# A cosine-attention and token/channel-mixer kernel: the first batch's k loads on ACT's DMA queue, with a rearranged order list

## The chip, the cores and the metric

The kernel runs on one core of a Trainium2 chip. The core has a matrix engine (TensorE, PE in the profile, with its weight loads as PEld), VectorE (DVE), ScalarE (ACT), GpSimd (POOL) and SyncE (SP), which here issues DMA transfers and does nothing else. The metric is the device time of one execution in microseconds. Before the change three runs gave 263.96, 264.58 and 265.01; the median is 264.58 us.

## What is computed

Eight batches of 8 heads, 576 positions, 64 features per head. First a linear attention with cosine weights, then a token mixer and a channel mixer with a residual. The reference, cut to what matters:

```python
def phi(x, c, s):                       # c, s: cos and sin of pi/2 * pos / S
    r = np.maximum(x, 0.0)
    return np.concatenate([r * c, r * s], axis=-1)
q_p = phi(q, cos_w, sin_w); k_p = phi(k, cos_w, sin_w)
kv = np.einsum('bhsf,bhsd->bhfd', k_p, v)
z = np.sum(k_p, axis=2)
num = np.einsum('bhsf,bhfd->bhsd', q_p, kv)
den = np.einsum('bhsf,bhf->bhs', q_p, z)[..., None] + 1e-06
x = (num / den)                          # heads side by side: (8, 576, 512)

xt = x.transpose(0, 2, 1)
h = np.maximum(xt @ w_tok1, 0.0) @ w_tok2
u = x + h.transpose(0, 2, 1)
out = u + np.maximum(u @ w_ch1, 0.0) @ w_ch2
```

## The kernel before

The program is a list, `PLAN` (line 21 on), of 1189 items, carried out from first to last while the program is built. Each item calls a small function with its arguments; a letter names the engine: A for ACT, V for DVE, G for POOL, Y for SP. Every engine works through its own instructions in the order of this list and waits where a result is not there yet. So the list sets the order of each engine and of each DMA queue, and which engine does an elementwise step.

The 576 positions of a batch are nine to each of 64 rows; odd and even partitions hold different parts of them. `load_part(b, name, par, eng, h0, h1)` (line 369) loads batch b of q, k or v for the even (par 0) or odd (par 1) partitions, for heads h0 to h1, with one DMA from the queue of `eng`. For batch 0 each of q, k and v comes in four loads: two parts, each for heads 0 to 3 (the first half) and 4 to 7 (the second half), of 320 KB for part 0 and 256 KB for part 1. For later batches a load covers all 8 heads.

For a batch the steps are:

- `feat` and `rfeat` (lines 389 and 395): relu of q and k with a cosine, sine or tangent factor, into `qp` and `kp`; `vcast` and `vcast_half`: v to bf16. Batch 0 does these by halves of the heads.
- `q_half_mm`, `q_half_out` (batch 0) turn q by TensorE and copy it; later batches use `q_turn_mm`/`q_turn_out` or the DMA transpose `q_turn` from SP.
- `kv_half`, `kv_half_out` and `num_half`, or `kv`, `kv_out`, `num`: the two attention products. `x_hadd`, `x_hrec`, `x_hmul` (or `x_add`, `x_rec`, `x_mul`, all on DVE) divide by the denominator.
- `b1_half`, `uT_x`, `uT_h`, `uT_out` (batch 0) or `b1`, `u_mm`, `u_out`, `u_cast`, `u_turn`: the token mixer. `u_mm(b, c)` makes half of u, `u_out` adds x, `u_cast` makes bf16, and the DMA transpose `u_turn` brings it to the layout for the channel mixer. Batch 0 gets that layout from TensorE (`uT_*`), and its `u_mm` serves the residual.
- `m1(g, s)` (line 805) and `m1_out`: the first channel product of group g, 12 slices of 4 matmuls with 512 columns. `m2` for group 0, and `h_sum`, `prod`, `quarter`, `seed` for the others: the second product with seven partial products in place of eight. Groups 0 to 7 are the batches; group 8 gathers the ninth positions (`tail_*`).

In the list the work of batch b+1 (features, attention, token mixer) lies between the channel products of group b. `warm(n)` (line 588) multiplies a tile of zeros into a PSUM bank n times; its result is not used. There are 28 such items with n = 2.

The weights come by `wtok_part(0..4)` (line 560, the two token matrices), `wc1_load` (line 563) and `wc2_load` (line 582), all from SP, and are cast to bf16 by `w1_cast`, `w2_perm`, `w2t_perm`, `wc1_cast`, `wc2_cast`.

One load of batch 0 is not in the list: the first half of k part 1 goes out on ACT's queue in the setup (line 505), ahead of ACT's table load and of the cosine and sine tables (lines 529 and 530). The other eleven loads of batch 0 are in the list, on SP, in this order: q part 0, k 0, q 1, v 0, v 1 (first halves), q 1, q 0, k 1, k 0, v 0 (second halves), then two token weight parts, v 1 (second half), two more token weight parts, a first piece of `wc1`, and the last token weight part.

Of the kernel before, what the change touches and what calls it, by code (L numbers as in the profile page):

```python
# [21 lines left out]
    ("warm", 2), ("warm", 2), ("warm", 2), ("load_part", 0, "q", 0, "Y", 0, 4), ("load_part", 0, "k", 0, "Y", 0, 4),  # L22
    ("feat", 0, "k", 0, 0, "V", 0, 4), ("feat", 0, "k", 0, 2, "V", 0, 4), ("feat", 0, "q", 1, 4, "A", 0, 4),
    ("feat", 0, "k", 1, 4, "V", 0, 4), ("load_part", 0, "q", 1, "Y", 0, 4), ("rfeat", 0, "q", 4, 5, "A", 0, 4),
    ("load_part", 0, "v", 0, "Y", 0, 4), ("load_part", 0, "v", 1, "Y", 0, 4), ("warm", 2), ("warm", 2),
    ("vcast_half", 0, 3, "G"), ("warm", 2), ("load_part", 0, "q", 1, "Y", 4, 8), ("feat", 0, "k", 1, 3, "A", 0, 4),
    ("feat", 0, "k", 0, 3, "V", 0, 4), ("q_half_mm", 0, 2), ("feat", 0, "q", 1, 1, "V", 0, 4),
    ("rfeat", 0, "q", 2, 4, "A", 0, 4), ("warm", 2), ("load_part", 0, "q", 0, "Y", 4, 8), ("warm", 2), ("warm", 2),
    ("warm", 2), ("feat", 0, "k", 1, 2, "V", 0, 4), ("feat", 0, "k", 0, 1, "A", 0, 4),
    ("feat", 0, "k", 1, 1, "A", 0, 4), ("feat", 0, "q", 1, 3, "V", 0, 4), ("vcast_half", 0, 1, "V"),  # L30
    ("load_part", 0, "k", 1, "Y", 4, 8), ("vcast_half", 0, 2, "G"), ("load_part", 0, "k", 0, "Y", 4, 8),
    ("rfeat", 0, "q", 0, 2, "A", 0, 4), ("warm", 2), ("feat", 0, "q", 1, 0, "V", 0, 4), ("q_half_mm", 0, 0),
    ("load_part", 0, "v", 0, "Y", 4, 8), ("q_half_out", 0, 2, "V"), ("wtok_part", 4),
    ("feat", 0, "q", 1, 2, "V", 0, 4), ("warm", 2), ("warm", 2), ("warm", 2), ("feat", 0, "k", 1, 0, "A", 0, 4),
    ("warm", 2), ("feat", 0, "k", 0, 4, "V", 0, 4), ("feat", 0, "q", 1, 1, "V", 4, 8), ("q_half_out", 0, 0, "V"),
    ("q_half_mm", 0, 1), ("feat", 0, "k", 0, 0, "V", 4, 8), ("wtok_part", 2), ("warm", 2), ("warm", 2),
    ("rfeat", 0, "q", 4, 5, "V", 4, 8), ("feat", 0, "k", 1, 3, "V", 4, 8), ("feat", 0, "q", 1, 2, "A", 4, 8),
    ("vcast_half", 0, 0, "A"), ("kv_half", 0, 0), ("kv_half", 0, 1), ("load_part", 0, "v", 1, "Y", 4, 8),
    ("vcast_half", 1, 1, "G"), ("kv_half", 0, 2), ("kv_half", 0, 3), ("vcast_half", 0, 4, "V"), ("kv_half", 0, 4),
    ("rfeat", 0, "q", 2, 4, "A", 4, 8), ("feat", 0, "k", 0, 2, "A", 4, 8), ("feat", 0, "q", 1, 4, "A", 4, 8),  # L40
    ("feat", 0, "q", 1, 0, "V", 4, 8), ("feat", 0, "k", 0, 3, "A", 4, 8), ("feat", 0, "k", 1, 2, "A", 4, 8),
    ("rfeat", 0, "q", 0, 2, "V", 4, 8), ("q_half_mm", 1, 0), ("wtok_part", 0), ("wtok_part", 1),
    ("w1_cast", 2, 4, "G"), ("warm", 2), ("feat", 0, "q", 1, 3, "A", 4, 8), ("q_half_out", 0, 1, "V"),
    ("q_half_mm", 1, 2), ("feat", 0, "k", 0, 4, "V", 4, 8), ("kv_half_out", 0, "V"), ("num_half", 0, 2),
    ("feat", 0, "k", 0, 1, "A", 4, 8), ("w2t_perm", 1, "V"), ("q_half_out", 1, 0, "V"), ("vcast_half", 1, 0, "V"),
    ("wc1_load", 0, 0, 256), ("num_half", 0, 1), ("num_half", 0, 0), ("wtok_part", 3), ("q_half_mm", 1, 1),
    ("vcast_half", 1, 2, "V"), ("feat", 0, "k", 1, 4, "V", 4, 8), ("w1_cast", 4, 5, "G"), ("vcast_half", 1, 3, "V"),
    ("warm", 2), ("wc1_load", 2), ("warm", 2), ("warm", 2), ("w2_perm", 1, 1, "V"), ("x_hadd", 0, 2),
    ("x_hadd", 0, 0), ("w1_cast", 0, 2, "G"), ("x_hadd", 0, 1), ("w2_perm", 0, 0, "A"), ("wc1_load", 1),
    ("x_hrec", 0, 1), ("feat", 0, "k", 1, 0, "A", 4, 8), ("kv_half", 1, 0), ("feat", 0, "k", 1, 1, "V", 4, 8),  # L50
    ("kv_half", 1, 1), ("kv_half", 1, 2), ("x_hrec", 0, 0), ("kv_half", 1, 3), ("q_half_out", 1, 1, "A"),
    ("x_hmul", 0, 0), ("load_part", 1, "k", 0, "Y"), ("wc1_cast", 8, "G"), ("vcast_half", 1, 4, "A"),
    ("kv_half", 1, 4), ("x_hmul", 0, 1), ("warm", 2), ("warm", 2), ("kv_half_out", 1, "A"), ("num_half", 1, 0),
    ("num_half", 1, 1), ("load_part", 1, "k", 1, "Y"), ("x_hrec", 0, 2), ("x_hmul", 0, 2), ("x_hadd", 1, 0),
    ("x_hrec", 1, 0), ("w2_perm", 1, 0, "G"), ("x_hadd", 1, 1), ("q_half_out", 1, 2, "A"), ("num_half", 1, 2),
    ("x_hadd", 1, 2), ("x_hrec", 1, 1), ("x_hrec", 1, 2), ("warm", 2), ("x_hmul", 1, 0), ("b1_half", 0, 0),
    ("w2_perm", 0, 1, "G"), ("b1_half", 0, 1), ("b1_half", 0, 2), ("b1_half", 0, 3), ("b1_half", 0, 4),
    ("b1_half", 1, 0), ("uT_x", 0), ("b1_half_out", 0, "A"), ("wc1_cast", 0, "A"), ("wc1_load", 0, 256, 512),
    ("wc1_cast", 10, "A"), ("b1_half", 1, 1), ("x_hmul", 1, 1), ("b1_half", 1, 2), ("load_part", 1, "q", 1, "Y"),
    ("uT_x", 2), ("b1_half", 1, 3), ("x_hmul", 1, 2), ("wc1_cast", 7, "A"), ("uT_x", 1), ("b1_half", 1, 4),  # L60
    ("uT_h", 0), ("b1_half_out", 1, "V"), ("wc1_cast", 9, "V"), ("wc1_cast", 1, "G"), ("uT_h", 1), ("uT_x", 3),
    ("uT_h", 3), ("uT_out", 0, "A"), ("load_part", 1, "q", 0, "Y"), ("uT_h", 2), ("wc1_cast", 11, "G"),
    ("uT_out", 1, "A"), ("uT_out", 2, "V"), ("u_mm", 0, 1), ("w2t_perm", 0, "V"), ("load_part", 1, "v", 0, "Y"),
    ("u_out", 0, 1), ("uT_out", 3, "A"),

    ("m1", 0, 7), ("load_part", 1, "v", 1, "Y"), ("m1_out", 0, 7, "V"), ("m1", 0, 1), ("feat", 1, "k", 1, 1, "V"),
    ("m1", 0, 9), ("wc1_cast", 4, "A"), ("feat", 1, "k", 0, 3, "A"), ("feat", 1, "k", 1, 3, "A"),
    ("wc1_cast", 5, "V"), ("feat", 1, "k", 1, 4, "A"), ("feat", 1, "k", 1, 0, "V"), ("m1_out", 0, 9, "V"),
    ("wc1_cast", 3, "G"), ("m1", 0, 11), ("m1_out", 0, 11, "V"), ("feat", 1, "k", 0, 1, "V"), ("m1_out", 0, 1, "A"),
    ("wc1_cast", 6, "G"), ("u_mm", 0, 0), ("m1", 0, 10), ("u_out", 0, 0), ("m1_out", 0, 10, "V"), ("wc2_load", 0),  # L70
    ("wc1_cast", 2, "G"), ("wc2_load", 1), ("feat", 1, "k", 0, 0, "A"), ("m1", 0, 5), ("vcast", 1, 0, "G"),
    ("feat", 1, "k", 1, 2, "A"), ("m1_out", 0, 5, "A"), ("m1", 0, 2), ("vcast", 1, 4, "G"), ("vcast", 1, 3, "G"),
# [214 lines left out]
def kernel(  # L287
# [17 lines left out]
    P = 128  # L305
# [4 lines left out]
    HH = H // 2  # L310
# [7 lines left out]
    A, V, G, SY = nc.scalar, nc.vector, nc.gpsimd, nc.sync  # L318
# [3 lines left out]
    def sb(name, shape, dt):  # L322
        return const.tile(shape, dt, name=name)
# [586 lines left out]
```

## Time and profile before

| | |
|---|---|
| median of the timed runs | 264.58 us (263.96 to 265.01) |
| profiled execution, its own time | 266.13 us |
| span of that execution in the profile | 264.4 us |
| mean granted TensorE clock | 0.992 of full speed |
| first `m1` matmul | 29.23 us |
| last matmul issued | 259.33 us, with 1.47 us to the end of its group of 12 |
| HBM read / written | 35.85 MB / 9.44 MB |

The profile is a record of one execution. Its page gives for each engine the busy time, for 40 slices of the span the busy share, and the groups of instructions with the idle time before them and what ended it. The trace behind it can be asked for single stretches, in order of time or as busy sums, and for the chain that ended last: that is followed back from the last instruction, at each step to whatever released it. "Idle time before" counts only time directly before an instruction. A line number of a helper (such as 373 for all `load_part` DMAs, or 379 for all casts) stands for many callers, so tile names tell them apart. The 40 slices (6.6 us each) for PE, the clock and the DMA engines are:

```
PE   7599999999999999999999999999999999999994
PEclk9899999999999999999999999999999999999999
DMA  5979999989999999999999999658534133200315
```

### The profile page before, as it was taken

The page shows a single profiled execution, that of the slowest core. Times are in us where ns is not written, and L with a number is a line of the kernel's source. Part 1 is how long each engine was busy: PE and PEld are TensorE (multiplying, and loading weights), DVE is VectorE, ACT ScalarE, POOL GpSimd, SP SyncE. Part 2 cuts the span into 40 slices and gives each one's busy share as a digit, 9 for nine tenths or more (in the row PEclk, how much of TensorE's full clock was granted, in tenths as well). Part 3 has the DMA queues.
Part 4 walks back from the last instruction along what each step waited for, and adds up shares of the span by engine and source line. Part 5 has one row for each costly group of instructions (what it writes and reads, how often), then busy time and mean ns, then how long its engine had stood idle before and what let it go on. Part 6 is the DMA issues. An engine that isn't in the chain of part 4 may idle for free.

```text
span 264.4 us, 5482 instructions
## 1 busy us (share of the span) xinstructions
PE 253.9 (96%) x2105; PEld 161.4 (61%) x2122; DVE 193.2 (73%) x400; ACT 130.9 (50%) x224; POOL 92.8 (35%) x100
## 2 busy tenths in 40 slices
PE   7599999999999999999999999999999999999994
PEld 3267456545458655774577457755775575567583
DVE  4677898787699587678898859679956775462574
ACT  3565876881598087855715862387212321222310
POOL 5114315169519201850740224421620160243030
PEclk9899999999999999999999999999999999999999
DMA  5979999989999999999999999658534133200315
GB/s 175 340 281 328 387 398 383 376 214 147 329 356 246 176 319 379 207 209 299 317 278 183 288 236 318 143 191 221 120 87 110 64 70 90 94 9 2 119 45 195
DMA packets 81818, 57.70 MB, mean 218 GB/s; under 512 B 50304, under 2 KB 76544, under 8 KB 81792
## 3 DMA queue, kind: packets, MB, share of 16 engines
q1 hardware_dynamic: 81088, 56.57, 77.3%
q10 hardware_dynamic: 704, 0.79, 0.9%
q8 instruction: 16, 0.26, 0.4%
q14 instruction: 10, 0.08, 0.1%
HBM read 35.85 MB, written 9.44 MB: 171 GB/s over the span
## 4 chain that ended last, share of the span: by engine, by line
PE 68%; DMA 17%; DVE 7%; ACT 3%; issue 3%; SPq 2%; DVEq 0%; ACTq 0%
PE psM L809 26%; PE psM L455 25%; DMA q_raw<-in_q_dram 5%; PE psA L754 5%; DMA u_sb<-in_moe_w_ch_dram 4%; PE psA L766 4%; DMA qpT<-qp 4%; PE psA L715 2%; DMA h1T<-in_moe_w_tok_dram 2%; PE psA L729 2%; DMA uT<-u_bf 2%; SPq L373 2%; ACT kp L401 1%; ACT qp L401 1%; DVE h1T L385 1%
## 5 line engine op out<-in xcount | busy, mean ns | idle before, releaser
L809 PE MATMUL psM<-uT,w_ch 128*128 128x512 bf16 x384 | 89.1, 379 | 0.4 <-ACT h1T L383 0.3
L383 ACT ACTIVATE h1T<-psM 128x512 bf16<-128x512 f32 x67 | 38.5, 595 | 60.5 <-PE psM L809 53.2
L809 PEld LDWEIGHTS <-w_ch 128*128 128x128 bf16 x432 | 40.7, 98 | 43.6 <-issue 0.4
L444 POOL TENSOR_TENSOR h1s<-h1T,h1s 128x512 bf16<-128x512 bf16 (+1 forms) x17 | 28.4, 1675 | 50.5 <-ACT h1T L383 44.2
L455 PEld LDWEIGHTS <-h1s 128*128 128x128 bf16 x384 | 37.2, 98 | 7.1 <-DVE h1s L444 0.2
L467 DVE TENSOR_TENSOR u_sb<-psM,u_sb 128x512 f32<-128x512 f32 x42 | 28.2, 683 | 17.7 <-PE psM L455 17.5
L379 POOL CAST vb<-v_raw 128x512 bf16<-128x512 f32 (+1 forms) x22 | 14.6, 694 | 56.0 <-DMA v_raw<-in_v_dram 50.5
L385 DVE TENSOR_SCALAR h1T<-psM 128x512 bf16<-128x512 f32 x41 | 27.6, 683 | 7.7 <-PE psM L809 7.3
L455 PE MATMUL psM<-w_ch2t,h1s 128*128 128x256 bf16 x276 | 33.1, 273 | 0.0
L455 PEld LDWEIGHTS <-h1T 128*128 128x128 bf16 x288 | 27.6, 98 | 5.4
L401 ACT ACTIVATE qp<-q_raw,tan_t 128x512 bf16<-128x512 f32 (+1 forms) x32 | 21.7, 689 | 10.2 <-DMA q_raw<-in_q_dram 5.9
L770 DVE TENSOR_TENSOR u_sb<-psA,x_sb 128x1024 f32<-128x1024 f32 x16 | 19.2, 1218 | 6.1 <-PE psA L766 3.7
L455 PE MATMUL psM<-w_ch,h1T 128*128 128x256 bf16 x192 | 23.6, 273 | 0.0
L744 DVE TENSOR_TENSOR x_sb<-psA,rden 128x512 bf16<-128x512 f32 x28 | 19.0, 685 | 0.6
L401 ACT ACTIVATE kp<-k_raw,cos_t 128x512 bf16<-128x512 f32 (+1 forms) x26 | 17.3, 679 | 3.0 <-DMA k_raw<-in_k_dram 3.0
L401 ACT ACTIVATE kp<-k_raw,sin_t 128x512 bf16<-128x512 f32 (+1 forms) x26 | 17.0, 673 | 3.2 <-DMA k_raw<-in_k_dram 3.2
L591 PE MATMUL psM<-wz 128*128 128x512 bf16 x52 | 15.8, 439 | 1.3 <-DVE wz L502 1.2
L444 POOL TENSOR_TENSOR h1s<-h1T 128x512 bf16<-128x512 bf16 x12 | 14.0, 1174 | 6.7 <-DVE h1T L385 6.7
L729 PEld LDWEIGHTS <-qpT 128*128 128x128 bf16 x280 | 12.5, 98 | 5.8 <-DMA qpT<-qp 1.0
L383 ACT ACTIVATE qp<-q_raw 128x512 bf16<-128x512 f32 (+2 forms) x17 | 13.4, 786 | 4.5 <-DMA q_raw<-in_q_dram 4.0
L766 PE MATMUL psA<-B,w_tok 128*128 128x512 bf16 x61 | 15.1, 379 | 0.2
L444 DVE TENSOR_TENSOR h1s<-h1T 128x512 bf16<-128x512 bf16 (+1 forms) x20 | 13.9, 707 | 1.5 <-ACT h1T L383 1.1
(125 smaller groups left out, 334.6 us busy)
## 6 DMA issues: line engine op xcount, KB each, us to landing
out_dram<-u_sb SPq DMA_DIRECT2D x32, 256.0 KB, 2.9
k_raw<-in_k_dram SPq DMA_DIRECT2D x7, 640.0 KB, 6.2
q_raw<-in_q_dram SPq DMA_DIRECT2D x7, 640.0 KB, 7.4
v_raw<-in_v_dram SPq DMA_DIRECT2D x7, 640.0 KB, 6.0
k_raw<-in_k_dram SPq DMA_DIRECT2D x7, 512.0 KB, 5.9
q_raw<-in_q_dram SPq DMA_DIRECT2D x7, 512.0 KB, 6.5
v_raw<-in_v_dram SPq DMA_DIRECT2D x7, 512.0 KB, 6.8
u_sb<-in_moe_w_ch_dram SPq DMA_DIRECT2D x2, 1024.0 KB, 9.0
```

Source lines behind the costliest of these rows:

```text
L383: eng.activation(out_ap, in_ap, AF.Relu)
L385: eng.tensor_relu(out_ap, in_ap)
L401: eng.activation(dst, src, AF.Relu, bias=0.0, scale=s)
L444: eng.tensor_tensor(out=o[:, k0:k1], in0=a[:, k0:k1], in1=b_[:, k0:k1], op=op)
L455: nc.tensor.matmul(bank[:, t * HC:(t + 1) * HC], lhs[:, ki, t * P:(t + 1) * P], rhs[:, ki, :], start=(first and ki == 0 and t == 0), stop= ...
L467: V.tensor_add(u, bank2(bank)[:, ts, :], u)
L591: nc.tensor.matmul(ps, wz[:, 0:P], wz, start=True, stop=True)
L729: nc.tensor.matmul(ps[:, h // HH, (h % HH) * E1:(h % HH + 1) * E1], qpT[:, h, j, :], kv_sb[:, h, 0:E1], start=True, stop=True, skip_group_ ...
L744: V.tensor_mul(dst.rearrange("p (g h d) -> p g h d", g=2, h=HH), heads(b, j)[:, :, :, 0:D], bcast(rden[j], [[HH, 2], [1, HH], [0, D]]))
L766: nc.tensor.matmul(ps[:, half, :], w2[:, ki, 2 * c + half, :], B1[b % 2][:, ki, :], start=(ki == 0), stop=(ki == NT - 1))
L770: V.tensor_add(u_sb[b % 2][:, 2 * c:2 * c + 2, :], of(("u", b, c)), x_sb[:, 2 * c:2 * c + 2, :])
L809: nc.tensor.matmul(ps.rearrange("p (t k) -> p t k", k=P), wc1[:, ki, s * P:(s + 1) * P], src[:, :, ki, :], start=(ki == 0), stop=(ki == NC ...
```

## The change

The first and second halves of k of batch 0, in both parts, are all loaded from ACT's queue. Part 0's first half joins part 1's first half in the setup; the two second halves are now the first loads of the list and name A. SP keeps the loads of q and v. The list has 1188 items: the same work as before, without the load that moved to the setup, in a new order throughout. About 230 items name another engine (for instance `u_cast` on POOL goes from 7 to 2 items, on ACT from 5 to 10). No function is changed or added.

```diff
     load_part(0, "k", 1, A, 0, HH)
+    load_part(0, "k", 0, A, 0, HH)
     pos_i = sb("pos_i", [P, 1], I32)
...
 PLAN = (
-    ("warm", 2), ("warm", 2), ("warm", 2), ("load_part", 0, "q", 0, "Y", 0, 4), ("load_part", 0, "k", 0, "Y", 0, 4),
-    ("feat", 0, "k", 0, 0, "V", 0, 4), ("feat", 0, "k", 0, 2, "V", 0, 4), ("feat", 0, "q", 1, 4, "A", 0, 4),
...
-    ("load_part", 0, "k", 1, "Y", 4, 8), ("vcast_half", 0, 2, "G"), ("load_part", 0, "k", 0, "Y", 4, 8),
...
-    ("uT_out", 1, "A"), ("uT_out", 2, "V"), ("u_mm", 0, 1), ("w2t_perm", 0, "V"), ("load_part", 1, "v", 0, "Y"),
-    ("u_out", 0, 1), ("uT_out", 3, "A"),
-
-    ("m1", 0, 7), ("load_part", 1, "v", 1, "Y"), ("m1_out", 0, 7, "V"), ("m1", 0, 1), ("feat", 1, "k", 1, 1, "V"),
...
+    ("load_part", 0, "k", 1, "A", 4, 8), ("feat", 0, "k", 0, 2, "V", 0, 4), ("load_part", 0, "k", 0, "A", 4, 8),
+    ("load_part", 0, "q", 0, "Y", 0, 4), ("feat", 0, "q", 1, 4, "A", 0, 4), ("load_part", 0, "q", 1, "Y", 0, 4),
+    ("feat", 0, "q", 1, 3, "V", 0, 4), ("load_part", 0, "v", 0, "Y", 0, 4), ("load_part", 0, "v", 1, "Y", 0, 4),
...
+    ("warm", 2), ("warm", 2), ("warm", 2), ("feat", 0, "k", 0, 4, "V", 0, 4), ("load_part", 0, "q", 0, "Y", 4, 8),
...
+    ("warm", 2), ("warm", 2), ("warm", 2), ("load_part", 0, "q", 1, "Y", 4, 8), ("feat", 0, "k", 1, 0, "V", 0, 4),
+    ("wtok_part", 3), ("q_half_mm", 0, 1), ("warm", 2), ("load_part", 0, "v", 1, "Y", 4, 8),
+    ("load_part", 0, "v", 0, "Y", 4, 8), ("warm", 2), ("feat", 0, "q", 1, 0, "A", 0, 4),
...
+    ("wtok_part", 4), ("wtok_part", 1), ("w1_cast", 4, 5, "G"), ("feat", 0, "k", 0, 1, "A", 4, 8),
+    ("wc1_load", 0, 0, 256), ("kv_half_out", 0, "A"), ("num_half", 0, 0), ("q_half_out", 0, 2, "V"),
...
+    ("uT_x", 3), ("uT_h", 3), ("uT_h", 2), ("uT_out", 0, "V"), ("uT_out", 2, "V"), ("u_mm", 0, 1), ("uT_out", 3, "V"),
+    ("wc1_cast", 0, "V"), ("u_mm", 0, 0), ("wc1_cast", 8, "A"), ("u_out", 0, 0),
+
+    ("m1", 0, 1), ("m1_out", 0, 1, "V"), ("u_out", 0, 1), ("m1", 0, 8), ("m1_out", 0, 8, "A"),
...
+    ("h_sum", 8, 3, 0, 6, "G"), ("prod", 8, 3, (0,)), ("quarter", 8, 2), ("prod", 8, 3, (1,)), ("warm", 2),
```

The new order of the loads on SP is: q part 0, q 1, v 0, v 1 (first halves), q 0, q 1 (second halves), a token weight part, v 1, v 0 (second halves), the other four token weight parts, then the pieces of `wc1`. In the list before, 24 `warm` items stand ahead of the first `m1` and 4 behind it; in the new one 25 and 3, and the last of these stands behind the last product. `u_mm(0, 0)` stood behind the fourth `m1` and now stands ahead of the first.

## The prediction, made before the changed kernel ran

> **What bounds the kernel now.** I read the engine totals first, then busy time by stretch, then the chain that ended last, and last the first 23 us in order of time. The totals say TensorE:
>
> ```profile
> span 264.4 us, 5482 instructions
> PE 253.9 (96%) x2105; PEld 161.4 (61%) x2122; DVE 193.2 (73%) x400; ACT 130.9 (50%) x224; POOL 92.8 (35%) x100
> ```
>
> The rows by stretch (length, then PE's busy us, then the other engines) show where its other 10.5 us lie:
>
> ```profile
> 5.00:10.00 5.00, 3.01 (x17) 1.12 (x14) 1.93 (x7) 2.11 (x5) 0.00 (x0) 1.00 0.93 293
> 10.00:15.00 5.00, 3.46 (x16) 1.86 (x17) 3.92 (x14) 4.08 (x11) 0.92 (x2) 0.66 1.06 386
> ...
> 60.00:90.00 30.00, 29.34 (x267) 18.50 (x267) 23.91 (x46) 16.19 (x28) 19.14 (x11) 1.00 1.09 259
> ...
> 125.00:150.00 25.00, 24.67 (x223) 16.58 (x224) 22.19 (x43) 13.81 (x23) 9.93 (x10) 1.00 1.09 261
> ...
> 225.00:264.40 39.40, 35.81 (x255) 24.76 (x253) 20.54 (x35) 8.26 (x15) 9.37 (x7) 0.99 0.21 77
> ```
>
> From 28.7 us to PE's last matmul (ends 260.8) the stretches add up to 1.8 us of idle PE, 0.66 of them between 60 and 90; behind 260.8 stand 3.6 us of a last add and the stores. So a change can gain in two ways: reach the first m1 (29.2 us) sooner, or put less PE work behind it. The first 29 us hold warm matmuls that compute nothing, so there PE's busy time is no measure. The chain that ended last runs through loads:
>
> ```profile
> 5.41 6.71 DMA q_raw<-in_q_dram
> 12.14 5.98 DMA h1T<-in_moe_w_tok_dram
> ...
> 21.09 1.29 DVE x_sb L647 x2
> ...
> 23.42 1.46 PE psM L657 x12
> ```
>
> That is: q's last half landed at 12.1, token weights at 18.1, and then features, normalising and b1. ACT's own rows there:
>
> ```profile
> 4.89 0.51 ACT L401 ACTIVATE qp<-q_raw,tan_t 128x256 bf16<-128x256 f32 x1 [1.22 <-DMA q_raw<-in_q_dram]
> 9.11 0.63 ACT L383 ACTIVATE qp<-q_raw 128x512 bf16<-128x512 f32 x1 [1.65 <-DMA q_raw<-in_q_dram]
> 9.64 0.49 ACT L401 ACTIVATE kp<-k_raw,cos_t 128x256 bf16<-128x256 f32 x1
> 10.04 0.49 ACT L401 ACTIVATE kp<-k_raw,sin_t 128x256 bf16<-128x256 f32 x1
> 21.71 0.38 ACT L377 CAST kv_sb<-psM 128x260 bf16<-128x260 f32 x1 [0.96 <-PE psM L601]
> ```
>
> ACT does little before 9.1 us. Half features lie 0.40 us apart back to back (9.64, 10.04) though one takes 0.49. The second half's kv cast ends at 22.1; from there to m1 it is 7.1 us.
>
> **The change part by part.** *Three k loads leave SP for ACT.* An issue takes 0.62 us on SP; SP loses 1.9 us. I count that as 0: from 2.25 us on the DMA engines are 86 to 93% busy, so SP's issues were ahead of the data. If that cover were gone, SP's 1.9 us would be the most to gain. The 17 first loads still bring 4.8 MB. The Trainium skill (DMA: Bandwidth & Descriptors, "Issuing engines are not separate DMA queues") says that issuing from several engines saves the issue time and nothing else, since all run on the same DMA engines; if that is all, the front gains nothing, which is the first rival below. The shares of 86 to 93% agree with it so far.
>
> *What ACT pays.* In the built kernel's instruction list every load takes one of eight completion semaphores in turn and waits for that semaphore's previous load. k part 1's second half waits for its first half (4.0 us: issued 0.73, 3.3 us to landing); k part 0's second half waits for q part 1's first half, and every ACT feature stands behind it. In the trace that q load was issued at 2.77 and landed at 9.05. SP will issue it at about 2.1, but k part 0 runs beside it: I take 8.4, with 7.5 and 9.05 as the ends. An issue on ACT took 0.72, so ACT's first feature starts at 9.1 instead of 4.9. That cover was mostly idle: ACT did only three features (1.4 us) before 9.1.
>
> *ACT's list from there to the second kv cast*: 7 half features (6 x 0.40 + 0.31 for a narrow one), a q copy 1.0, a wait for q's last half, then 0.52 + 3 x 0.40 + 2 x 0.40, the first kv cast 0.3, 0.4, a v cast 0.3, 2 x 0.40 + 0.31, two q copies of 0.9, the kv cast 0.38. q's last half lands when its bytes come up: 2.87 MB stand before it, k's included; the trace had moved that much at 11.9 us and landed loads about 2 us after, so 13.9; ACT gets there at 12.8. 13.9 + 6.8 = 20.7 for the end of the cast, against 22.1: a gain of 1.4. With 0.50 for each feature (its duration, not its spacing) the sum is 22.1, a gain of 0. Between these ends I take 0.8, towards the spacing row since the features do stand back to back, less something for DVE, which has to deliver the last cosine feature at 18.3 after its own queue.
>
> *The token weights.* The last of their five loads was issued at 18.54, behind a DVE cast, and DMA was only 20% busy from 18.0 to 20.25. The new list issues all five ahead of their casts, and channel weights directly after. Worth nothing at the first m1 by itself, as its casts are POOL's and were not last; it moves about 2.25 x 0.8 = 1.8 us of transfers forward, which may shorten the loads waited for between 40 and 64 us. I count 0 and keep it in the range.
>
> *PE work moved.* u_mm of c 0 now precedes the first m1 (0.86 us, 4 matmuls at 0.216, from the chain's 1.73 for 8). It shifts m1 and takes the same off what follows: 0. Of 28 warm entries (2 matmuls, 0.43 us each) 4 stood behind the first m1; now 3 do, one of them after the last product, where the stores outlast it. Two fewer on the bound engine: -0.86.
>
> *The rest of the list* is rearranged for all batches, and some 230 items change engine. Bounds: at best the 1.8 us of idle PE go; at worst see the DVE rival. Counting from the lists, the distance in PE work from the last u_cast to the m1 that needs it (a DMA transpose of 4.4 us lies between) was 0.2 us in two batches before (POOL casts) and is 1.3 to 8.3 now; DVE's load in the groups of batches 2 to 4 is 74.8 us against 67.8. One helps, one hurts; I take 0.
>
> Sum: 0 - 0.8 - 0.86 = -1.7 us. The profiled execution measured 266.13 around its span of 264.4; the three timed runs have a median of 264.58. The span would be 262.7, and the same difference on the median gives **262.9**.
>
> **Rivals.** *The front gains nothing.* Loads bring the same bytes at the same rate, and ACT's wait for q eats its lead. For it: DMA at 93% in the row of 5 to 10 us, and the rule above. Against: q's and v's last halves no longer queue behind token weights. If q part 1 lands at 9.05 and features take 0.50, the cast ends up to 0.7 us later than 22.1; with the warm entries' -0.86 the time is 263.7 to 264.4. No change.
>
> *DVE becomes the bound in batches 3 and 4: slower.* For the group of batch 4 I count on DVE 7 adds, 7 reciprocals, 5 x_mul, 6 quarters, 6 features, 5 m1_out, 2 u_out, 3 h_sum and 6 others: 24.7 us beside 25.4 of PE (before: 19.9); for batch 3 26.6 beside 28.0. Where DVE was fullest, from 125 to 150, it still idled 25 - 22.19 = 2.8 us in waits for others. If it needs that again, the groups last 27.5 and 29.4: +2.1 and +1.4. It decides from the point where DVE's count passes PE's less 2.8. That gives 262.9 + 3.5 = 266.4. Against it: before, batch 3 had 28.4 beside 28.0, and PE idled only 0.33 there, since neighbouring groups lent time.
>
> *More than forecast.* The front gains its full 1.4 and the earlier weights remove 1.0 of the 1.8 idle: 264.58 - 1.4 - 0.86 - 1.0 = 261.3.
>
> That the loads do not move is excluded by the built list, which has them on ACT.
>
> **How the numbers follow.** Forecast 0.34 (own range 262.2 to 263.6), more than forecast 0.12, front gains nothing 0.25, DVE or another engine as a new bound 0.29. A measurement can tell about 0.5%, 1.3 us, from no change: faster is below 263.3, slower above 265.9. Faster: most of the forecast's own range and all of the case above it, 0.42; within: the flat case and the forecast's upper edge, 0.29; slower: 0.29. The range runs from 261.0 (the larger gain) to 266.6 (the DVE case); outside I leave 0.2, mostly above, where a wait that no list shows would lie.
>
> **What would show it.** Right: ACT's first feature near 9.1 us; kv cast of the second half ending near 20.7; the first m1 near 28.7 to 29.4 with both u_mm behind it; two fewer warm matmul pairs after it; DMA busy through 18 to 20 us; idle PE from there to the end near 1.8. Wrong on the front: the cast at 22 or later, with ACT waiting for q or k loads in the rows just before. Wrong on the rest: more than 3 us of idle PE after the first m1, released by DVE's h_sum, x_mul or m1_out in the rows of batches 3 and 4, or by transposes. The forecast fails if q part 1 lands after 9.7, or if SP's queue stops at batch 1's loads.

## The result, and the profile after

Over 22 runs of each kernel the changed one took a median of 263.80 us (262.83 to 264.46), the one before 264.74 (263.96 to 267.85). The ratio is 0.9954 with a 95% interval of 0.9938 to 0.9970: about 1.2 us, or 0.46%, faster. (Ratios and intervals, here and below, leave out an execution that is more than 1.5% above the fastest of its kernel; medians and ranges count all.) The prediction was 262.9, with 261.0 to 266.6 as its range.

The page of the changed kernel opens with its span and the engines' totals:

```profile
span 262.1 us, 5484 instructions
PE 254.6 (97%) x2122; PEld 160.5 (61%) x2122; DVE 193.0 (74%) x401; ACT 134.9 (51%) x226; POOL 89.3 (34%) x97
```

Its own time was 263.85 us, 0.05 from its median. That was not so for the kernel before: its first profile stood at 266.13, 1.4 us above the median of 264.74. So the two profiles differ by 2.3 us where the medians differ by 0.9, and a second profile of the kernel before (run `before_again`, below) is needed to read the difference. The busy time by stretch, with the columns as before (length, PE, PEld, DVE, ACT, POOL, granted clock, DMA share, GB/s):

```profile
5.00:10.00 5.00, 5.00 (x27) 2.43 (x26) 2.17 (x7) 1.87 (x5) 0.94 (x3) 1.00 1.03 346
10.00:15.00 5.00, 4.86 (x55) 2.70 (x54) 4.12 (x14) 5.00 (x13) 0.96 (x3) 1.00 1.07 403
60.00:90.00 30.00, 28.81 (x256) 17.93 (x253) 25.03 (x50) 17.40 (x27) 11.82 (x8) 1.00 1.02 268
```

In the front PE is almost always busy now and holds its full clock, the DMA engines carry 346 GB/s from 5 to 10 us (293 in the first profile of before, 340 in the second), and ACT is full from 10 to 15. From 60 to 90 us, though, PE idles 1.19 us, where it idled 0.66 (0.26 in the second profile): something was gained at the start and given back later. The front in order of time on ACT (start, duration, engine, line; idle time before in brackets):

```profile
3.93 4.07 ACTq L372 DMA_DIRECT2D k_raw<-in_k_dram  x2
8.13 0.51 ACT L400 ACTIVATE qp<-q_raw,tan_t 128x256 bf16<-128x256 f32 x1 [4.08 <-DMA q_raw<-in_q_dram]
...
18.53 0.38 ACT L376 CAST kv_sb<-psM 128x260 bf16<-128x260 f32 x1
...
19.60 0.66 ACT L376 CAST w_tok<-h1T 128x256 bf16<-128x256 f32 x1
```

The two issues of k's second halves hold ACT for 4.07 us, as the prediction said they would, until q part 1 has landed. The second half's kv cast ends at 18.91 us; it was predicted for 20.7 and stood at 22.09 before. In the list before, ACT had waited 1.99 us for a cast of token weights, `w2_perm(0, 0)`, ahead of its last k feature:

```profile
18.21 0.68 ACT L377 CAST w_tok<-h1T 128x256 bf16<-128x256 f32 x1 [1.99 <-DMA h1T<-in_moe_w_tok_dram]
```

In the new list POOL does this cast. The one that ACT does at 19.60 is another, `w2_perm(0, 1)`; it comes behind the kv cast and waits for nothing. The chain that ended last shows the same:

```profile
2.11 5.26 DMA q_raw<-in_q_dram
7.39 0.61 ACTq L372
...
24.97 1.73 PE psA L766 x8
```

No token weight (h1T) is in it any more. From 10.99 us on it is PE alone, up to the first m1 at 26.54 us. That is with both `u_mm` ahead of it, 0.86 us of which came later in the list before: counted alike, m1 is reached 29.23 + 0.86 - 26.54 = 3.5 us sooner than in the first profile of before. The new list ends PE's work with a pair of warm matmuls:

```profile
257.06 1.47 PE L454 MATMUL psM<-w_ch,h1s 128*128 128x256 bf16 x12
258.37 0.59 PE L591 MATMUL psM<-wz 128*128 128x512 bf16 x2
```

The end of the last product is what counts: 258.53 now, 260.80 before, so 2.3 us sooner, and 3.6 us of the span stand behind it in both. From the first m1 to the last product it is 232.0 us; before it was 231.6, of which 1.7 us (one `u_mm`, two pairs of `warm`) are gone. So the new list loses 232.0 - (231.6 - 1.7) = 2.1 us behind the first m1. PE's waits there (waiting for, in total, times, longest):

```profile
PE psA L702 <- DVE qp L402: 1.1, 1, 1.1
PE psM L809 <- DMA uT<-u_bf: 0.8, 1, 0.8
PE psM L454 <- POOL h1s L443: 0.5, 1, 0.5
PE psA L729 <- DMA qpT<-qp: 0.4, 1, 0.4
PE psA L754 <- DVE x_sb L744: 0.2, 1, 0.2
```

These are 3.0 us. In the profile of before the waits behind the first m1 add up to 1.0 (0.5 for qpT, 0.3 for h1T, 0.2 for x_sb); the difference of 2.0 is about the loss.

### The profile page after: what moved, and what is told of

Its sections match the earlier page's. It is cut to its first block, busy times and chain, and to the rows that moved or that the text cites. A ratio compares the mean times of both kernels' runs of the same rounds, so it can differ in the third digit from the quotient of the medians.

```text
span 262.1 us, 5484 instructions
## 1 busy us (share of the span) xinstructions
PE 254.6 (97%) x2122; PEld 160.5 (61%) x2122; DVE 193.0 (74%) x401; ACT 134.9 (51%) x226; POOL 89.3 (34%) x97
## 4 chain that ended last, share of the span: by engine, by line
PE 71%; DMA 11%; DVE 10%; ACT 3%; issue 2%; POOL 1%; ACTq 0%; SPq 0%; DVEq 0%; POOLq 0%
PE psM L809 26%; PE psM L454 22%; DMA q_raw<-in_q_dram 5%; PE psA L754 5%; PE psA L766 4%; DMA k_raw<-in_k_dram 3%; PE psA L729 3%; PE psA L715 2%; DMA uT<-u_bf 2%; PE psM L591 2%; DVE kp L402 2%; PE psM L821 2%; ACT kp L400 2%; DMA qpT<-qp 2%; DVE qp L402 1%
## 5 line engine op out<-in xcount | busy, mean ns | idle before, releaser
L809 PE MATMUL psM<-uT,w_ch 128*128 128x512 bf16 x384 | 90.2, 379 | 0.8 <-DMA uT<-u_bf 0.8
L382 ACT ACTIVATE h1T<-psM 128x512 bf16<-128x512 f32 x71 | 40.9, 595 | 68.9 <-PE psM L809 63.8
L384 DVE TENSOR_SCALAR h1T<-psM 128x512 bf16<-128x512 f32 x37 | 25.1, 686 | 16.6 <-PE psM L809 10.6
L466 DVE TENSOR_TENSOR u_sb<-psM,u_sb 128x512 f32<-128x512 f32 x42 | 28.1, 682 | 11.9 <-PE psM L454 11.5
L378 POOL CAST vb<-v_raw 128x512 bf16<-128x512 f32 (+1 forms) x23 | 13.5, 618 | 61.2 <-DMA v_raw<-in_v_dram 48.6
L443 POOL TENSOR_TENSOR h1s<-h1T 128x512 bf16<-128x512 bf16 (+1 forms) x11 | 17.7, 1616 | 31.8 <-DVE h1T L384 16.8
L744 DVE TENSOR_TENSOR x_sb<-psA,rden 128x512 bf16<-128x512 f32 x28 | 18.9, 686 | 0.7
L400 ACT ACTIVATE qp<-q_raw,tan_t 128x512 bf16<-128x512 f32 (+1 forms) x25 | 16.2, 673 | 4.9 <-DMA q_raw<-in_q_dram 4.1
L400 ACT ACTIVATE kp<-k_raw,sin_t 128x512 bf16<-128x512 f32 (+1 forms) x24 | 15.7, 663 | 5.6 <-PE psA L715 4.5
L376 ACT CAST u_bf<-u_sb 128x1024 bf16<-128x1024 f32 x10 | 10.4, 1044 | 10.6 <-DVE u_sb L770 8.6
L754 PE MATMUL psA<-x_sb,w_tok 128*128 128x512 bf16 x56 | 14.5, 379 | 0.2 <-DVE x_sb L744 0.2
L400 ACT ACTIVATE kp<-k_raw,cos_t 128x512 bf16<-128x512 f32 (+1 forms) x22 | 14.5, 673 | 0.2 <-DMA k_raw<-in_k_dram 0.2
```

The lines of the kernel that those rows point to most:

```text
L382: eng.activation(out_ap, in_ap, AF.Relu)
L384: eng.tensor_relu(out_ap, in_ap)
L400: eng.activation(dst, src, AF.Relu, bias=0.0, scale=s)
L443: eng.tensor_tensor(out=o[:, k0:k1], in0=a[:, k0:k1], in1=b_[:, k0:k1], op=op)
L466: V.tensor_add(u, bank2(bank)[:, ts, :], u)
L754: nc.tensor.matmul(ps[:, mi, :], w1[:, j, mi * P:(mi + 1) * P], rhs, start=(j == 0), stop=(j == NJ - 1))
```

## The experiments

Ratios are to the kernel before, run on the same chip in the same group of runs.

| run | what it is | median us | ratio (95%) | first m1 | last product ends |
|---|---|---|---|---|---|
| before (first profile) | | 264.74 | | 29.23 | 260.80 |
| after | | 263.80 | 0.9954 (0.9938 to 0.9970) | 26.54 * | 258.53 |
| queue_only | old list, k on ACT's queue | 264.60 | 0.9976 (0.9952 to 1.0000) | 28.47 | 258.93 |
| order_only | new list, k on SP's queue | 263.39 | 0.9941 (0.9919 to 0.9963) | 26.43 * | 258.10 |
| front_new_rest_old | new list to the first m1, then the old | 265.57 | 1.0016 (0.9990 to 1.0041) | 26.95 * | 259.47 |
| front_old_rest_new | old list to the first m1, then the new | 265.39 | 1.0010 (0.9985 to 1.0035) | 29.27 * | 259.66 |
| before_again | old list, second profile | one run, 263.74 | | 27.77 | 258.42 |
| token_load_early | old list, last token load issued earlier | 265.50 | 1.0009 (0.9982 to 1.0037) | 28.71 | 260.22 |
| token_casts_late | old list, two token weight casts later | 263.48 | 0.9929 (0.9892 to 0.9966) | 26.77 | 256.21 |
| front_new_rest_old2 | as the third, one cast at the seam moved | 265.27 | 1.0007 (0.9983 to 1.0030) | 28.53 * | 260.73 |
| casts_late_again | token_casts_late, repeated | 263.73 | 0.9939 (0.9907 to 0.9972) | 26.57 | 258.42 |
| casts_late_queue | token_casts_late with k on ACT's queue | 265.98 | 1.0039 (1.0016 to 1.0061) | 27.79 | 260.55 |
| after_cast_back | new list, one token cast back in its old place | 266.98 | 1.0083 (1.0054 to 1.0112) | 28.91 * | 261.79 |
| after_q_first | new list, one VectorE feature moved up | 263.56 | 0.9938 (0.9920 to 0.9956) | 26.61 * | 258.21 |

A star marks lists in which both `u_mm` of batch 0 stand ahead of the first m1. The last two columns are of one profiled execution each.

### The queue alone, and the order alone

`queue_only` is the list before with only the loads changed:

```diff
     load_part(0, "k", 1, A, 0, HH)
+    load_part(0, "k", 0, A, 0, HH)
 PLAN = (
+    ("load_part", 0, "k", 1, "A", 4, 8), ("load_part", 0, "k", 0, "A", 4, 8),
...
-    ("load_part", 0, "k", 0, "Y", 0, 4),
...
-    ("load_part", 0, "k", 1, "Y", 4, 8),
...
-    ("load_part", 0, "k", 0, "Y", 4, 8),
```

> The list of before, with only the three k loads moved to ACT's queue (part 0's first half in the setup, the two second halves at the head of the list). Queue theory (two queues keep the DMA engines fuller, and that is what brought the first m1 from 29.2 to 26.5 us): DMA share from 4.5 to 9 us rises from 0.86 to 0.93 in before to about 1.0, q's last half lands by 11.2 instead of 12.1, the first m1 comes by 28.2, time 0.4 to 0.8% below before. List theory (the queue is worth nothing by itself; the order of loads and features is): DMA share as before, ACT's first q feature waits until about 8.1 instead of 4.9, first m1 at 29 to 30, time equal to before or up to 0.5% above.

`order_only` is the changed list with the three loads back on SP: k part 0 behind q part 0, the two second halves behind q part 1's.

> The list of after, with the three k loads back on SP: k part 0's first half right behind q's, the two second halves behind q's second halves, all else as after. Queue theory: DMA share from 4.5 to 9 us falls back to about 0.9, first m1 at 28 or later, time at or above before. List theory: first m1 within 0.7 us of after's 26.5, time 0.3 to 0.6% below before, like after's.

The queue alone is worth at most half a per cent and possibly nothing (0.9976, up to 1.0000). The list without the queue change has the whole gain (0.9941, where the full change has 0.9954; the two can't be told apart). In `queue_only` the DMA engines and ACT look like this (rows by stretch, then rows in time):

```profile
4.50:6.75 2.25, 1.23 (x5) 0.35 (x3) 0.05 (x1) 0.00 (x0) 0.00 (x0) 1.00 1.01 351
6.75:9.00 2.25, 0.34 (x4) 0.35 (x5) 1.90 (x8) 1.21 (x4) 0.18 (x1) 0.83 1.07 372
9.00:11.25 2.25, 2.25 (x9) 0.87 (x7) 1.74 (x7) 2.25 (x6) 0.89 (x2) 0.50 1.07 397
```

```profile
4.11 3.55 ACTq L372 DMA_DIRECT2D k_raw<-in_k_dram  x2
7.79 0.51 ACT L400 ACTIVATE qp<-q_raw,tan_t 128x256 bf16<-128x256 f32 x1 [3.74 <-DMA k_raw<-in_k_dram]
...
14.11 0.51 ACT L400 ACTIVATE kp<-k_raw,cos_t 128x256 bf16<-128x256 f32 x1 [1.65 <-DMA k_raw<-in_k_dram]
...
16.52 0.64 ACT L376 CAST w_tok<-h1T 128x256 bf16<-128x256 f32 x1
```

From 4.5 to 9 us the bytes do come sooner, 351 and 372 GB/s where the two profiles of before had 259 and 293, and 295 and 355. But ACT, which issues two of the loads, stands in the issue until 7.7 us and starts its features at 7.79 instead of 4.9, PE idles meanwhile, and its granted clock falls to 0.50. Then it waits 1.65 us more for k's second half, until 14.11. The token weights have landed by the time it arrives at their cast, at 16.52, so the 2 us that it waited there before are gone. Waits ahead of the cast took the place of the wait for it.

### A second profile of before

> The kernel before, unchanged, profiled a second time: its first profile's own time stood 1.4 us above its median. Theory: the excess of that profile is chance in the front (the first m1 at 29.2 us); a second profile has its own time near 264.7, a span of 262.9 to 263.3 and the first m1 at 28.0 to 28.6. Rival: the excess is spread over the batches behind; then the first m1 is again 29.1 to 29.4 and the last matmul ends near 259.5.

Its own time was 263.74 us, its span 262.0, the first m1 came at 27.77, all of them below what either text gave. This execution was 1.3 us faster than the median of its group (265.01), the first 1.4 us slower than the median of its own: the typical front lies between the two. So the front of the same list differs by 1.5 us between two executions, because the loads land differently: q part 1, for which ACT's feature waited until 9.11 in the first profile, was there by 7.28 in the second. What does not differ is ACT's wait for token weights:

```profile
14.25 0.49 ACT L401 ACTIVATE kp<-k_raw,cos_t 128x256 bf16<-128x256 f32 x1
16.76 0.65 ACT L377 CAST w_tok<-h1T 128x256 bf16<-128x256 f32 x1 [2.02 <-DMA h1T<-in_moe_w_tok_dram]
17.31 0.50 ACT L401 ACTIVATE kp<-k_raw,sin_t 128x256 bf16<-128x256 f32 x1
...
20.25 0.38 ACT L377 CAST kv_sb<-psM 128x260 bf16<-128x260 f32 x1 [1.23 <-PE psM L601]
```

The cast `w2_perm(0,0,"A")` waits 2.02 us for loads, and behind it, in ACT's order, stands the last k feature that the second kv product needs. The cast's own result is not wanted before 24 us. The load that ends the wait isn't even the one that the cast reads. Its weights come with the load of 576 KB, issued in the first profile of before at 9.10 and landed 6.9 us later, at 16.0, before ACT came free at 16.2. But that load and those of the other token matrix write one tile (`h1T`), and in the built program the cast waits for three of them. The last was a load of 256 KB, issued at 12.14 and landed 6.0 us later, at 18.1.

Against this profile, whose kv cast ends at 20.63 and whose last product ends at 258.42, the new front is 27.77 + 0.86 - 26.54 = 2.1 us better, and the new rest loses 231.99 - (230.65 - 1.72) = 3.1 us.

### The token weights: their load or their casts

The prediction had named the gap in the loads at 18 us (DMA share 0.20). `token_load_early` closes it in the list before:

```diff
-    ("wtok_part", 0), ("wtok_part", 1),
+    ("wtok_part", 0), ("wtok_part", 1), ("wtok_part", 3),
```

> The list before with one load moved: the last token weight part is issued with the others instead of behind VectorE's cast. Theory (the front is bound by ScalarE's and VectorE's work and waits, not by how early the weights come): the share of the DMA engines from 18 to 20.25 us rises from 0.20 to 0.9 or more, the first m1 stays within 0.4 us of 29.2, time 0 to -0.8 us. Rival (the gap in the loads is what cost the front its time): the first m1 moves to 28.0 or before and the time falls by 1.0 us or more.

```profile
18.00:20.25 2.25, 1.58 (x10) 0.74 (x9) 2.22 (x11) 1.33 (x3) 0.65 (x2) 1.00 1.05 383
```

The share rose to 1.05, the first m1 lay at 28.71, between the two profiles of before, and the time did not change (1.0009). ACT still waited 2.00 us ahead of its token cast, until 17.07. The load that was moved is a part of 64 KB of the other token matrix, and none of the three that this cast waits for. So the run tests the gap in the loads, and not an earlier end of the cast's wait. `token_casts_late` moves the early casts out of the way instead:

```diff
-    ("w2t_perm", 1, "V"), ("q_half_out", 1, 0, "V"),
+    ("q_half_out", 1, 0, "V"),
...
-    ("x_hadd", 0, 1), ("w2_perm", 0, 0, "A"), ("wc1_load", 1),
+    ("x_hadd", 0, 1), ("wc1_load", 1),
...
-    ("q_half_out", 1, 2, "A"),
+    ("q_half_out", 1, 2, "A"), ("w2_perm", 0, 0, "A"),
...
-    ("w2t_perm", 0, "V"),
+    ("w2t_perm", 0, "V"), ("w2t_perm", 1, "V"),
```

> The list before with two casts of token weights moved: ScalarE's (w2_perm 0,0), for which it waited 2.0 us, goes behind the last half's q copy, and VectorE's (w2t_perm 1), for which it waited 0.5, goes beside the other w2t_perm. Theory (these waits held the second half's features): ScalarE has no wait over 0.5 us between 14 and 20 us, the second kv cast ends at 20.3 to 21.0 instead of 22.1, the first m1 comes at 27.3 to 28.3, the time falls by 0.6 to 1.6 us. Rival (the second halves of v or q, or VectorE, hold the front anyway): the first m1 stays at 28.7 or later and the time is within 0.4 us of before.

```profile
15.13 0.49 ACT L400 ACTIVATE kp<-k_raw,sin_t 128x256 bf16<-128x256 f32 x1
16.98 1.01 ACT L376 COPY qpT<-psM 128x1024 bf16<-128x1024 bf16 x1 [1.36 <-PE psM L687]
...
19.06 0.38 ACT L376 CAST kv_sb<-psM 128x260 bf16<-128x260 f32 x1 [0.77 <-PE psM L600]
...
19.81 0.68 ACT L376 CAST w_tok<-h1T 128x256 bf16<-128x256 f32 x1
```

The last k feature starts at 15.13 instead of 17.31 or 18.78, the kv cast ends at 19.44, the first m1 comes at 26.77, and the time falls by 0.7% (0.9929). The front gained somewhat more than the theory gave. Two waits for PE are left on ACT in this stretch, 1.36 us for the turned q and 0.77 for the kv product, where none above 0.5 was expected. Two items moved in a list of 1189 are worth as much as the whole change, as far as the intervals tell. The repetition agrees:

> token_casts_late once more, unchanged, for a narrower interval beside the next kernel. Theory (the two early token weight casts were the loss in the front of the kernel before): ratio to before 0.990 to 0.996 again, own time 261.5 to 263.5, first m1 26.5 to 27.3. Rival (the first result was chance in the loads): ratio above 0.997.

Measured: 0.9939, first m1 at 26.57. By the medians of all executions, 263.73 and 265.10, the ratio would be 0.995. Its executions spread widely, from 261.70 to 266.22; those of the changed kernel lay within 262.83 to 264.46.

The other way round, `after_cast_back` puts the first of these casts back in the changed list where it stood, on ACT ahead of the k features (the changed list has it on POOL):

```diff
-    ("feat", 0, "k", 1, 0, "A", 4, 8), ("wc1_load", 1),
+    ("w2_perm", 0, 0, "A"), ("feat", 0, "k", 1, 0, "A", 4, 8), ("wc1_load", 1),
...
-    ("w2t_perm", 0, "G"), ("w2_perm", 0, 0, "G"), ("w2_perm", 1, 0, "G"),
+    ("w2t_perm", 0, "G"), ("w2_perm", 1, 0, "G"),
```

> The changed kernel with one cast put back to where the list before had it: w2_perm(0,0) on ScalarE ahead of the second half's k features. Theory (this placement was the main loss): ScalarE waits 1.3 to 1.9 us for token weights near 15 us, the second kv cast ends at 20.6 to 21.4 instead of 18.9, the first m1 comes at 28.0 to 29.0 instead of 26.5, the time is 265.0 to 266.2 (ratio to before 1.001 to 1.005). Rival (the gain came from the new loads and the new order together): first m1 below 27.3, time within 0.5 us of after, 263.3 to 264.3.

```profile
14.73 0.36 ACT L376 CAST kv_sb<-psM 128x260 bf16<-128x260 f32 x1
16.72 0.66 ACT L376 CAST w_tok<-h1T 128x256 bf16<-128x256 f32 x1 [1.63 <-DMA h1T<-in_moe_w_tok_dram]
17.28 0.51 ACT L400 ACTIVATE kp<-k_raw,sin_t 128x256 bf16<-128x256 f32 x1
...
20.90 0.39 ACT L376 CAST kv_sb<-psM 128x260 bf16<-128x260 f32 x1
```

ACT waits 1.63 us for token weights and spends 0.56 on the cast, the second kv cast ends at 21.29 instead of 18.91, the first m1 is at 28.9, and the kernel is 0.8% slower than before: 1.0083 / 0.9954 = 1.013 against the changed kernel, 3.4 us. The theory gave 1.2 to 2.4 us. The front accounts for 2.4 us (28.91 - 26.54); a further 0.9 appears behind it (261.79 - 28.91 = 232.9 against 232.0). So the place of this cast decides whether the change gains or loses.

### The queue once the cast is out of the way

> token_casts_late with all k loads of batch 0 on ScalarE's queue, as the change has them: the queue's worth once the wait for token weights is gone. Theory (the queue is worth little either way, since ScalarE's first feature waits in it until 7.8 us): within 0.3% of casts_late_again, first m1 within 0.6 us of it. Rival (a second queue brings bytes earlier and this was hidden behind the token weights in queue_only): the first m1 at 26.0 or before, 0.8 us or more below casts_late_again in time.

Both failed. With k on ACT's queue, `token_casts_late` is slower, not equal and not faster: 1.0039 against 0.9939 in the same group, a ratio of 1.010, and 2.25 us between the medians. Rows of it on ACT:

```profile
3.97 3.21 ACTq L372 DMA_DIRECT2D k_raw<-in_k_dram  x2
7.31 0.51 ACT L400 ACTIVATE qp<-q_raw,tan_t 128x256 bf16<-128x256 f32 x1 [3.25 <-DMA k_raw<-in_k_dram]
...
11.65 0.51 ACT L400 ACTIVATE qp<-q_raw,tan_t 128x256 bf16<-128x256 f32 x1 [0.90 <-DMA q_raw<-in_q_dram]
...
13.96 0.51 ACT L400 ACTIVATE kp<-k_raw,cos_t 128x256 bf16<-128x256 f32 x1 [0.96 <-DMA k_raw<-in_k_dram]
...
20.27 0.38 ACT L376 CAST kv_sb<-psM 128x260 bf16<-128x260 f32 x1 [0.64 <-PE psM L601]
```

ACT starts 2.4 us later than in `casts_late_again` (7.31 against 4.95), but behind that it waits for loads again, 0.90 and 0.96 us: by 13.96 the late start is used up here too. What comes late is the data. The last load of k's second half was issued at 6.57, from SP in `casts_late_again` at 6.72; it took 7.3 us to land, from SP 5.6, and q's last loads took 6.4 and 6.8 us against 4.8 and 5.0. So the feature that needs k starts at 13.96 against 12.37. The kv cast ends at 20.65 against 19.10, the first m1 comes 1.2 us later, and PE, which waits 2.8 us for ACT's q feature until 8.18, is granted a clock of 0.66 and 0.58 in the rows from 6.75 to 11.25. The run gives the price of the second queue in this list as a whole; what the issue that holds ACT, the later landings and the lower clock cost one by one was not tried. In the changed list the same 4 us on ACT cost little: `order_only` starts its first ACT features at 4.89 and the next at 7.24, and its second kv cast ends at 18.79, against 18.91.

### Front and rest

`front_new_rest_old` joins the changed list up to the first m1 to the list before behind it; `front_old_rest_new` is the opposite. What one half had done already was left out of the other; what was missing was put at the seam.

> After's list up to the first m1, before's list from there on (four items that stood on the other side moved along; one warm pair more than in either, 29 in all). Theory that the list behind the first m1 gives back some 2 us: PE loses about 2.3 us behind the first m1, as in before, instead of about 4.4, and the time is 0.8 to 1.3% below before, the best so far. Rival, that the later stages are held by loads whatever the list is: the front's gain is lost again in waits for loads before 80 us, and the time is within 0.3% of after's.

> Before's list up to the first m1 (k loads as before), after's list from there on. Theory that the rest of the new list costs some 2 us of PE time: 0.4 to 0.8% above before. Rival, that later stages are held by loads: with the loads as late as before they hide the difference, and the time is within 0.3% of before's.

Neither gains (1.0016 and 1.0010). The first, however, made a wait of its own at the seam:

```profile
PE psM L809 <- DVE w_ch L378: 1.6, 1, 1.6
```

A weight cast stands there on DVE behind two additions of 1.22 us. `front_new_rest_old2` moved this cast to ACT, ahead of the first m1:

> As front_new_rest_old (the new list to the first m1, the old list behind it), with the one cast at the seam (wc1_cast 9), which held VectorE's queue there, on ScalarE and its load ahead of batch 1's v. Theory (the new front is worth about 2 us and the give-back belongs to the new rest): PE's 1.6 us wait for w_ch is gone, first m1 near 26.9, last matmul ends at 257.9 to 258.5, time 263.0 to 264.0. Rival (any rest gives the lead back, since batch 1's features have less room ahead of the products that need them): last matmul at 259.2 or later, time 264.6 or more.

It missed as well: 1.0007. PE now waited twice for weight casts on POOL, 1.8 us in all, and in its profile the front itself came late: the two `u_mm` start at 26.04, in the changed kernel at 24.81. So the two halves of a list can't be exchanged: weight casts, features and products are interleaved across the seam, and the two runs with the new front show the cost of a new seam as much as that of the halves. `front_old_rest_new` is different: PE has no such wait at its seam. From its first m1 to its last product it is 230.4 us, where the old rest, counted alike, has 229.9 or 228.9 (231.57 and 230.65, less 1.72). So behind the old front the new rest loses 0.5 or 1.5 us, in waits for a turned q (0.6), a transposed u (0.5) and POOL's sums (0.5). The wait of 1.1 us for a q feature on DVE, the largest of the changed kernel, is not among them. The rest of the 2.1 to 3.1 us therefore appears only with the early front. An early front alone costs nothing clear: in the two profiles of the kernel of `token_casts_late` it stood before the old rest, which took 229.4 and 231.9 us against 231.6 and 230.7 in before. All of these are single profiles, and those of one kernel differ by 0.9 and 2.4 us here, so the parts are rough.

### A part of what the rest gives back

The largest single wait behind the first m1 in the changed kernel is 1.1 us at 37.75, for a q feature on DVE. Features of that size on DVE, and what POOL does beside them, in the changed kernel:

```profile
29.61 1.27 DVE L402 TENSOR_SCALAR kp<-k_raw,cos_t 128x512 bf16<-128x512 f32 x3
...
32.78 0.84 DVE L402 TENSOR_SCALAR qp<-q_raw,tan_t 128x512 bf16<-128x512 f32 x1
33.54 0.83 DVE L402 TENSOR_SCALAR kp<-k_raw,sin_t 128x512 bf16<-128x512 f32 x1
...
36.78 0.82 DVE L402 TENSOR_SCALAR qp<-q_raw,tan_t 128x512 bf16<-128x512 f32 x1
```

```profile
32.04 2.05 POOL L378 CAST w_ch<-h1s 128x512 bf16<-128x512 f32 x2 [4.50 <-DMA h1s<-in_moe_w_ch_dram]
35.12 2.21 POOL L378 CAST vb<-v_raw 128x512 bf16<-128x512 f32 x3 [1.03 <-DMA v_raw<-in_v_dram]
37.60 1.41 POOL L378 CAST w_ch<-w_ch2t 128x512 bf16<-128x512 f32 x2 [0.27 <-DMA w_ch2t<-in_moe_w_ch_dram]
```

DVE is solidly busy from 29.6 to 38 us, and the q feature (36.78, ends 37.60) stands behind two k features and a weight cast. `after_q_first` moves it ahead of them:

```diff
-    ("q_turn_out", 1, 1, "V", "P"), ("wc2_load", 1), ("feat", 1, "k", 1, 3, "V"),
+    ("q_turn_out", 1, 1, "V", "P"), ("feat", 1, "q", 1, 0, "V"), ("wc2_load", 1), ("feat", 1, "k", 1, 3, "V"),
```

> The changed kernel with one VectorE feature moved up: the q feature for which PE waits 1.1 us at 37.75 goes ahead of two k features and a weight cast that stood before it on VectorE. Theory (part of the lead is given back there because VectorE is full and its order puts this one late): that wait is gone, a wait of 0.2 to 0.6 for a k feature may take its place, the last matmul ends at 258.0 to 258.6 instead of 258.96, time 0.3 to 0.9 us below after (263.80). Rival (VectorE is the bound of this stretch, so the wait only moves): PE waits the same 1.0 us for k features ahead of kv, no change within 0.3 us.

```profile
PE psA L729 <- DMA qpT<-qp: 0.9, 1, 0.9
PE psM L454 <- POOL h1s L443: 0.8, 1, 0.8
PE psM L809 <- DMA uT<-u_bf: 0.6, 1, 0.6
PE psM L809 <- DVE w_ch L378: 0.5, 1, 0.5
```

The wait for qp is gone; 0.5 us for the weight cast that is now later on DVE came in its place, and the transposes and POOL's sums hold PE a little longer in the batches behind. The last product ends 0.3 us sooner, just short of what the theory gave. In time it is 263.56 (0.9938) beside 263.80 (0.9954) for the changed kernel: in the right direction, but the intervals overlap. Of the 1.1 us about 0.3 was gained; the rest of the wait only moved.

## Why the prediction came out as it did

The direction was right and the time lay in the range, 0.9 us above the forecast. Its sum was -0.8 for the front, -0.86 for the warm pairs and 0 for the rest. By the two profiles of before (29.23 and 27.77 for the first m1) it was -3.5 or -2.1, -0.86, and +2.1 or +3.1, which adds up to the differences of the spans, -2.3 and +0.1. Two of its terms were far off and had opposite signs: that the time still lay in the range is luck.

- *The own time of the profile.* The prediction carried the difference between profile and median over unchanged. The 1.5 us were in the front, where the same list runs differently from one execution to the next, and the rows from which the front was worked out were those of a late one.
- *Three loads leave SP, counted as 0.* Right for SP. The rule from the Trainium skill (DMA: Bandwidth & Descriptors, "Issuing engines are not separate DMA queues"), that issuing from several engines saves only the time to issue, holds here as to what a second queue saves. The DMA share from 4.5 to 9 us was 0.86 and 0.93 in the first profile of before, 0.95 and 1.03 in the second, 1.01 and 1.07 with the queue alone; yet the queue alone gave no clear gain, and in `casts_late_queue` a loss. The rival that went with the rule, "the front gains nothing", is what `queue_only` did; it was not what the change did, since the change has another list.
- *ACT's wait for q part 1.* The mechanism was right: its first feature stood behind the issue of k part 0, until q's first half had landed. It landed at 7.4, not 8.4, and the feature started at 8.13, not 9.1. The price was counted as covered, because ACT did little before 9 us. In the changed list it was, and in `queue_only` other waits stood in its place. In `casts_late_queue` the queue as a whole cost 2.25 us, but there too ACT waited for loads again behind its late start, so this is not the price of the held issue alone.
- *ACT's list to the second kv cast, -0.8.* This is the step that was mis-sized. It was worked out as a sum over the new list with a wait in it, for q's last half until 13.9. That wait did not occur. The half was issued at 4.10 and 4.76 and landed 6.4 and 6.3 us later, by 11.1; ACT came to it at 12.1, straight from its own work. (Eight features stand ahead of the q copy there, not seven; the assumed wait hid that.) The features stood 0.40 us apart as taken, so with 12.1 in place of 13.9 the sum gives 18.9, as measured. The 13.9 rested on the first profile of before, in which 2.87 MB had moved at 11.9 us; by the rows of 2.25 us the second profile had moved them at 11.0, the changed kernel at 10.9. Besides, 0.8 was taken instead of the sum's own 1.4, on account of a lower end of 0 that does not come out: with 0.50 for each feature the sum gives 21.7, a gain of 0.4. What the prediction did not see is what had made the old list long: the 2 us wait for a token weight cast in front of a k feature. It quoted the load of h1T from the chain of before (12.14, 5.98 us), but not ACT's row at 18.21 with its 1.99 us of waiting for it. Of the token weights it said only that their earlier issue was "Worth nothing at the first m1 by itself, as its casts are POOL's and were not last"; that a cast on ACT had left the path of the k features was not in the sum. `token_casts_late` and `after_cast_back` show that it is the largest single term of the front that a run took apart.
- *The token weights issued earlier, 0.* Right: `token_load_early` filled the gap and gained nothing.
- *u_mm ahead of m1, 0, and two warm pairs fewer, -0.86.* Both as the list says; no run took them by themselves.
- *The rest, 0.* Wrong: +2.1 to +3.1 us. The bound of -1.8 was on the gain side and the price above was taken from the DVE rival in batches 3 and 4. That rival did not occur: behind 105 us PE waits 0.2 us for DVE. The losses are a DVE feature in batch 1 (1.1 us), a transpose of u (0.8), POOL's h_sum (0.5) and a transpose of q (0.4). `after_q_first` removed the first of them and got 0.3 us of it. Behind the old front the new rest lost 0.5 or 1.5 us. Which of its items cost the remainder behind the early front stays open.

Of what was to show it: the kv cast (20.7 forecast, 18.91), the first m1 (28.7 to 29.4 forecast, 26.54) and the idle PE behind it (1.8 forecast, 3.07 summed over the stretches from 28 to 150 us) were all missed, the first two to the good. The mark for "wrong on the rest", more than 3 us, was just reached in its amount, though the largest wait was in batch 1 and not in batches 3 and 4. The DMA engines were busy from 18 to 20 us (1.05), and two warm pairs fewer stand between the first m1 and the last product, as forecast.

The version with the lowest median is the changed list with k's loads on SP (`order_only`, 263.39). The list before with two casts moved is as good by its ratios (0.9929 and 0.9939), and so is the changed list with one feature moved up (0.9938). All of these lie below the full change's 0.9954, and all of their intervals overlap with its own, so that none is shown to be faster. The old list's early casts moved and the new list's other gains were not joined in one kernel, nor were the warm matmuls taken out of the new front, where PE alone now makes up the chain.

## What to carry to other kernels

Ahead of an engine's queue of moved loads, look for the instruction in that engine's own order which waits for data that nobody needs yet, with needed work behind it: a row of the kind "idle 2.0 us, released by a DMA" on an engine whose next instruction is on the path. Here moving the instruction mended it, and filling the gap in the loads did not; whether an earlier load, or a tile of its own for the load that the cast reads, would have done so was not tried. Before an engine that computes issues a load, look whether the issue will have to wait: here two issues held ACT for 3.2 to 4.1 us, which the changed list covered, while in another list the second queue cost 2.25 us. And when a list is arranged anew as a whole, count front and rest apart, up to the last matmul whose result is used, from more than one profile of the kernel before.

## What the runs showed of the hardware

Three features of 128x512 take DVE 1.27 us back to back while POOL is idle (29.61), and a single one 0.48 (31.17 in the first profile of before, where POOL is idle until 31.65). While POOL casts from f32 to bf16 run beside them, they take 0.82 to 0.84 (32.78, 33.54, 36.78), and POOL's casts take 0.7 to 1.0 us each instead of 0.61. The Trainium skill (SBUF — State Buffer, "Who interferes with whom") says that VectorE in its two-port mode and GpSimd share a port pair as an exclusive lock, so that the second to come is blocked until the first is done. The rows agree in that a feature is lengthened by 0.35 us, less than a whole cast. That POOL is the cause was not tried by itself; it is read from the coincidence in time, in this kernel, in `after_q_first` (34.97, 0.84) and in before (31.89, 0.84 beside a cast on POOL; 33.85, 0.47 after POOL's last). Whether these features run in the two-port mode no row shows.

The granted clock of PE in the front depends on how the loads land: where PE idled for about 3 us (2.9 in `queue_only`, 2.8 in `casts_late_queue`, 3.2 in the first profile of before) it fell to 0.50, 0.58 and 0.50 in the rows behind; a wait of 2.1 us in `token_casts_late` and one of 1.4 in `before_again` left it at 1.00, as did the changed list, whose front has no wait of that length. The changed kernel's 22 runs lie within 1.6 us, those of before within 3.9.
